# A ring of two small query tiles in place of two big ones, and one more row sum, in a fused attention backward pass

## The chip, the cores and the metric

The kernel runs on one core of a Trainium2 chip. A core has a matrix engine (PE; its weight loads are listed as PEld), a vector engine (DVE), a scalar engine (ACT), a general engine (POOL), and SyncE (SP), which here only issues transfers. Each works through its own list of instructions in order and waits at semaphores for the others. Transfers are carried out by 16 DMA engines that all queues share.

The metric is the device time of one execution in microseconds (us). A profiled execution gives two numbers: the span, from the first to the last instruction, and its own device time, which adds what lies around the span.

## What is computed

The reference is a forward pass of two attention blocks side by side and its gradient with respect to all eight inputs. S = 2048 tokens, D = 448, H = 16 heads of Dh = 28.

```python
# block A: linear attention, phi(t) = (t + 1 if t > 0 else exp(t)) + 1e-6
# block B: softmax attention with one key and value head for all 16 query heads
q = (x @ wq).reshape(B, S, H, Dh).transpose(0, 2, 1, 3);  k = x @ wk;  v = x @ wv
scores = einsum("bhqd,bkd->bhqk", q, k) * Dh ** -0.5
p = softmax(scores);  o = einsum("bhqk,bkd->bhqd", p, v)
out = concat([A(...), o.transpose(0, 2, 1, 3).reshape(B, S, H * Dh) @ wo], axis=-1)
# outputs: out, and the gradients of A_x, A_wqkv, A_wo, B_x, B_wq, B_wk, B_wv, B_wo
```

What follows concerns the backward pass of block B. With E = exp(scores), l the row sums of E, and dO the gradient of o: dP = dO vT, dS = E/l * (dP - D), where D is the row sum of dO * o. Then dQ = dS k, dK = dS^T q, dV = (E/l)^T dO.

## The kernel before

The kernel has two stages. The first (block A, and the projections of block B) takes about the first 200 us. The second is the core of block B, a loop over units u = 0 .. NU+27 with NU = 512 (lines 931 to 1049), and then a tail with the weight gradients and dX (lines 1051 to 1128). The order of the instructions inside the loop is the program's order; nothing reorders them.

A block b (64 of them) is a chunk of 256 queries, qc = b // 8, by a pair of heads, b % 8; two blocks share a group g of four heads. A unit is one eighth of a block: 256 of the 2048 keys, for two heads. Unit u does the scores S of block u // 8 and, 16 units behind, the dP of unit w = u - 16:

- `rows_SD` (L683) does the matmuls of S(u) and dP(w). ACT takes both halves of exp(S) into `eT` (L955, L997) and copies the second half of dP to `cp` (L971). DVE multiplies the first half of dP with `eT` into `dsT` (L967), POOL the second half (L972).
- After every fourth unit SP transposes four units of `eT` into `eN` with one DMA transpose of 128 x 4096 elements (L999). `dv_mm` (L901) reads `eN` for dV: block b in units 8b+20, 8b+22 and 8b+24. `eT` is a ring of five such tiles, `eN` of six.
- DVE transposes `dsT` in blocks of 32 into `dsx` (L1041), and `dk_m` (L865) multiplies it with the transposed queries `qX` for dK. Block b does so in the odd units 8b+27 to 8b+33.
- `o_norm` (L823) makes `rl` = 1/l and `don` = dO/l; its column 0 of each head carries D/l, which `row_D` (L833: one DVE reduction of `prod`, two small POOL multiplications) writes in unit 8b+12. `don_T` (PE, unit 8b+14) transposes `don` into `doT`, the operand of dP. A constant -1 in the values makes the matmul subtract D.
- dQ of block b is written over the block's queries in `qT_B`, in unit 8b+27 (L986).

The transposed queries. `qX` holds one 256-query chunk for all 16 heads, 128 x 8 x 512 elements, in two tiles that take turns (pools `cqXa` and `cqXb`). It is made group by group: `qc_copy` (L854, two calls for the even and the odd queries) spreads one group's queries into a staging tile, each repeated four times, and `qc_T` (L859) has SP transpose that, 128 x 1024 elements, into a quarter of `qX`. Chunk 0 is made ahead of the loop (L924 to L930), with `dsT` tiles as staging, one copy on POOL and one on DVE per group. Chunk c > 0 is made during the units of chunk c - 1: group g is copied by POOL in units 64(c-1) + 29 + 8g and the next one, into the single staging tile `qst`, and transposed at the end of the second. So in units 64(c-1)+29 to 64(c-1)+54 there is one group every 8 units, in the other units of a chunk there is none, and there is none from unit 448 on.

`row_D` is called inside `if hasD` (L963), which holds from unit 16 on. For block 0 it would be due in unit 12, so it isn't called, and column 0 of `don` stays what `o_norm` wrote, which is zero: block 0 is computed without D.

SP's list in the loop, in order: the load of `wo` (L923); the four transposes of chunk 0; then `eN` after every fourth unit; eight small transfers `put_shift` in unit 11 (L632); the transposes into `qX`; the transposes of `do_nat` into `oTq` (L1048) in units 130, 258, 386, 450 and 514. From unit 512 on `post_load` (L761, called at L1014) loads what the tail needs into `eT` tiles that are done: grad_out rows first (L775), then x rows (L780). `gwo` (L783), which starts in unit 520 on PE, multiplies with these rows; it is the last thing that PE does in its unit.

Of the kernel before, what the change touches and what calls it, by code (L numbers as in the profile page):

```python
# [11 lines left out]
BF16 = mybir.dt.bfloat16  # L12
# [5 lines left out]
P = 128  # L18
# [7 lines left out]
def kernel(  # L26
# [21 lines left out]
    nc = tc.nc  # L48
# [602 lines left out]
    with ExitStack() as cs_:  # L651
        pe_ = cs_.enter_context(tc.tile_pool(name="ceT", bufs=1, side="right"))
        pn_ = cs_.enter_context(tc.tile_pool(name="ceN", bufs=1, side="right"))
        pd_ = cs_.enter_context(tc.tile_pool(name="cdsT", bufs=5, side="right"))
        pqa_ = cs_.enter_context(tc.tile_pool(name="cqXa", bufs=1, side="right"))
        px_ = cs_.enter_context(tc.tile_pool(name="cdsx", bufs=2, side="right"))
        pqb_ = cs_.enter_context(tc.tile_pool(name="cqXb", bufs=1, side="right"))
        pc_ = cs_.enter_context(tc.tile_pool(name="ccp", bufs=3, side="right"))
        pw_ = cs_.enter_context(tc.tile_pool(name="cwk", bufs=4, side="right"))
        pp_ = cs_.enter_context(tc.tile_pool(name="cout", bufs=2, side="right"))  # L660
# [4 lines left out]
        dsT, dsx, qX, don, doT, rl, prod = ({} for _ in range(7))  # L665
# [3 lines left out]
        def eT(u):  # L669
            return ETs[u // 4 % 5][:, u % 4, :, :]  # L670
# [4 lines left out]
        def mmt(out, lhsT, rhs, pos, start, stop):  # L675
            nc.tensor.matmul(out, lhsT=lhsT, rhs=rhs, start=start, stop=stop, tile_position=pos,  # L676
                             skip_group_check=True)

        def blk(b):
            qc, pair = divmod(b, 8)  # L680
            return qc, pair, pair // 2, pair % 2
# [27 lines left out]
        qst = pp_.tile([P, 8, 4, 32], BF16, name="qst", bufs=1)[:, :, :, :]  # L709
# [92 lines left out]
        def due(u, lag):  # L802
            b, r = divmod(u - lag, 8)
            return b if r == 0 and 0 <= b < NB else None
# [28 lines left out]
        def row_D(b):  # L833
            Dq = pw_.tile([P, 2, 2, 1], F32, name="Dq")
            nc.vector.tensor_reduce(out=Dq[:, :, :, 0], in_=prod[b][:], axis=AX.X, op=ALU.add)
            nc.gpsimd.tensor_tensor(out=Dq[:], in0=Dq[:], in1=rl[b][:], op=ALU.mult)
            nc.gpsimd.tensor_tensor(out=don[b][:, :, :, 0:1], in0=Dq[:], in1=rl[b][:], op=ALU.mult)
# [13 lines left out]
            doT[b] = pw_.tile([P, 256], BF16, name="doT", bufs=2)  # L851
            nc.vector.tensor_copy(out=doT[b][r:r + 64, :], in_=tps2.pop(b)[r:r + 64, 0:256])  # L852

        def qc_copy(eng, st, qc, g, s):  # L854
            src = qT_B[g][:, qc * 256:(qc + 1) * 256].rearrange("p (b j s) -> p b j s", b=4, s=2)[:, :, :, s]
            eng.tensor_copy(out=st.rearrange("p (b s) a j -> p b s a j", s=2)[:, :, s, :, :],  # L856
                            in_=src.unsqueeze(2).to_broadcast([P, 4, 4, 32]))

        def qc_T(st, qc, g):  # L859
            nc.sync.dma_start_transpose(qX[qc].rearrange("p b s c -> p (b s) c")[:, :, g * P:(g + 1) * P],  # L860
                                        st.rearrange("p n a j -> p (n a j)"))

        dk_two = SB[2]

        def dk_m(b, m, other=0):  # L865
            qc, pair, g, hp = blk(b)
            h, B, s = m // 8, (m // 2) % 4, m % 2
            for a in range(4):
                rhs = dsx[b][32 * a:32 * a + 32, :, h, :, :].rearrange(
                    "p u t (b i s) -> p u t b i s", b=4, s=2)[:, :, :, B, :, s]  # L870
                k = 32 * ((a + 2) % 4) if other else 32 * a
                mmt((dk_two if other else dk_acc)[k:k + 32, :],
                    qX[qc][32 * a:32 * a + 32, B, s, pair * 64 + 32 * h:pair * 64 + 32 * h + 32],
                    rhs, (32 * a, k), other == 2 or b == 0 and m == 0, other == 0 and b == NB - 1 and m == 15)

        def o_mm(v):
# [44 lines left out]
        do_slots.update({32 + 8 * n: (13 + n // 4, n % 4 * P, n % 4 * P + P) for n in range(12)})  # L921
        with tc.manual_schedule():
            nc.sync.dma_start(wo, wo_d[:, 0:D].rearrange("(g p) c -> p g c", p=P))  # L923
            qX[0] = pqa_.tile([P, 4, 2, 512], BF16, name="qX")  # L924
            for g in range(4):
                st = pd_.tile([P, 2, 512], BF16, name="dsT").rearrange("p a (n j) -> p a n j", j=32).rearrange(
                    "p a (n b) j -> p (a n) b j", b=4)
                qc_copy(nc.gpsimd, st, 0, g, 0)
                qc_copy(nc.vector, st, 0, g, 1)
                qc_T(st, 0, g)  # L930
            for u in range(NU + 28):
                w = u - 16
                hasS = u < NU
# [5 lines left out]
                if u % 2 == 0:  # L939
                    b, n = divmod(u - 20, 8)  # L940
# [22 lines left out]
                if hasD:  # L963
                    dst = pd_.tile([P, 2, 512], BF16, name="dsT")
                    dsT[w] = dst
                    ew = eT(w)
                    nc.vector.tensor_tensor(out=dst[:, 0, :], in0=dp[0][:, :], in1=ew[:, 0, :], op=ALU.mult)  # L967
                    if (b := due(u, 12)) is not None:
                        row_D(b)
                    cp = pc_.tile([P, 512], BF16, name="cp")  # L970
                    nc.scalar.activation(out=cp[:, :], in_=dp[1][:, :], func=ACT.Copy)  # L971
                    nc.gpsimd.tensor_tensor(out=dst[:, 1, :], in0=cp[:, :], in1=ew[:, 1, :], op=ALU.mult)  # L972
                gq, iq = divmod(u % 64 - 29, 8)
                qq = u // 64 + 1
                if 0 <= gq < 4 and u < 448:
                    if gq == 0 and iq == 0:
                        qX[qq] = (pqb_ if qq % 2 else pqa_).tile([P, 4, 2, 512], BF16, name="qX")
                    if iq < 2:
                        qc_copy(nc.gpsimd, qst, qq, gq, iq)
                if u == 7:  # L980
                    nc.vector.memset(oTs[64:128, :], 0.0)
                if (b := due(u, 9)) is not None:
# [1 line left out]
                if (b := due(u, 27)) is not None:  # L984
                    qc, pair, g, hp = blk(b)
# [10 lines left out]
                if hasS:  # L996
                    nc.scalar.activation(out=eT(u)[:, 1, :], in_=sp[1][:, :], func=ACT.Exp, scale=scale)  # L997
                    if u % 4 == 3:
                        nc.sync.dma_start_transpose(ENs[u // 4 % 6][:, :, :],  # L999
                                                    ETs[u // 4 % 5][:, :, :, :].rearrange("p a b c -> p (a b c)"))  # L1000
                    if 0 <= gq < 4 and iq == 1 and u < 448:
                        qc_T(qst, qq, gq)

                if u % 2:
                    b, i = divmod(u - 27, 8)
                    if 0 <= b < NB:
                        for m in range(2 * i, 2 * i + 4):
                            dk_m(b, m, (1 + (u == 519 and m == 2 * i + 1)) * (m % 2) if 519 <= u < 537 else 0)
                else:
                    o_dq((u - 2, u - 1), (u - 20, u - 19))  # L1010
# [26 lines left out]
                if 0 <= y < NU:  # L1037
                    b, tp = divmod(y, 8)
                    if tp == 0:
                        dsx[b] = px_.tile([P, 8, 2, 2, 256], BF16, name="dsx")  # L1040
                    nc.vector.transpose(  # L1041
                        out=dsx[b][:, tp, :, :, :].rearrange("p h t c -> p (h t c)").bitcast(F32),
                        in_=dsT[y][:, :, :].rearrange("p h c -> p (h c)").bitcast(F32))
# [20 lines left out]
        for c in range(4):  # L1064
            t = dkvT[0:32, :].rearrange("p (t a i) -> p t a i", a=4, i=32)[:, :, c, :]
            src = dk_acc[32 * c:32 * c + 32, :].rearrange("p (t i) -> p t i", i=32)
# [93 lines left out]
```

## Time and profile before

| | us |
|---|---|
| median of 3 timed runs | 1042.17 (1039.36 to 1042.62) |
| device time of the profiled execution | 1044.09 |
| its span | 1042.4 |
| PE busy | 1003.5 (96%) |
| DVE, ACT, POOL busy | 886.9, 865.2, 812.3 |
| first exponential of the loop starts at | 207.09 |
| last exponential (unit 511) starts at | 969.45 |

The granted TensorE clock is full throughout. In a line of the profile that starts with a line number, the fields are: line, engine, operation, tiles written and read, shape, count, then busy time and the mean of one in ns, then the engine's idle time just before such instructions and what ended it. In a timeline the two numbers ahead of the engine are the start and the duration in us; SPq is SP's list of transfers, and a transfer's duration there is the time that SP takes to hand it over, not the time until it has landed.

### The profile page before, as it was taken

The numbers are of one execution on the slowest core, as the hardware profiler recorded it, in microseconds if no ns is written. First come the engines' busy times: TensorE is split into PE (matmuls) and PEld (weight loads), VectorE is DVE, ScalarE is ACT, GpSimd is POOL, SyncE is SP. The second block draws the span as 40 slices with busy tenths as digits, with TensorE's granted clock in tenths as the row PEclk, the third lists the DMA queues.
The fourth block names the chain that finished last, engine by engine and source line by source line (L and its number), as shares of the span: only waits on it lengthen the run. The fifth ranks groups of instructions, "written<-read, shape, count | busy, mean of one in ns | idle before, by whom it ended". The sixth has DMA issues, their size and how long they took to land.

```text
span 1042.4 us, 40109 instructions
## 1 busy us (share of the span) xinstructions
PE 1003.5 (96%) x16245; PEld 485.1 (47%) x16245; DVE 886.9 (85%) x1780; ACT 865.2 (83%) x1743; POOL 812.3 (78%) x1106
## 2 busy tenths in 40 slices
PE   9999999999999999999999999999999999999998
PEld 5555554434444444444444444444444444444444
DVE  7897500669999999999999999999999999999942
ACT  6463132599999999999999999999999999999632
POOL 8601282238998998999999989998999999889860
PEclk9999999999999999999999999999999999999999
DMA  9879999299999999999999999999999999999983
GB/s 261 157 137 191 176 229 218 38 161 201 194 187 192 187 193 194 202 187 194 201 193 195 192 187 204 198 182 202 188 197 186 195 195 195 200 188 203 228 168 90
DMA packets 689058, 195.15 MB, mean 187 GB/s; under 512 B 670408, under 2 KB 686688, under 8 KB 688872
## 3 DMA queue, kind: packets, MB, share of 16 engines
q1 hardware_dynamic: 680392, 179.97, 105.0%
q0 software_dynamic: 4544, 9.46, 3.0%
q10 hardware_dynamic: 3936, 3.16, 1.0%
q8 instruction: 127, 2.08, 0.8%
q14 instruction: 59, 0.48, 0.2%
HBM read 12.60 MB, written 10.84 MB: 22 GB/s over the span
## 4 chain that ended last, share of the span: by engine, by line
PE 39%; DVE 25%; POOL 16%; ACT 8%; issue 7%; DMA 3%; DVEq 0%; SPq 0%; ACTq 0%; POOLq 0%
PE agen L81 13%; POOL dsT L972 12%; DVE dsT L967 10%; PE agen L676 9%; DVE dsx L1041 9%; PE aacc L676 8%; PE aacc L81 7%; ACT cp L971 4%; ACT eT L997 2%; DMA eN<-eT 2%; DVE doT L852 1%; DVE R L986 1%; POOL qst L856 1%; POOL prod L821 1%; PE aacc L809 1%
## 5 line engine op out<-in xcount | busy, mean ns | idle before, releaser
L972 POOL TENSOR_TENSOR dsT<-cp,eT 128x512 bf16<-128x512 bf16 x512 | 584.6, 1156 | 49.4 <-ACT cp L971 42.6
L1041 DVE STREAM_TRANSPOSE dsx<-dsT 128x512 f32<-128x512 f32 x512 | 356.7, 697 | 5.8 <-POOL dsT L972 3.2
L676 PEld LDWEIGHTS <-R 32*128 32x128 bf16 (+1 forms) x9104 | 245.1, 94 | 243.3 <-issue 192.5
L967 DVE TENSOR_TENSOR dsT<-agen,eT 128x512 bf16<-128x512 f32 x512 | 340.3, 665 | 11.3 <-PE agen L676 5.4
L971 ACT ACTIVATE cp<-agen 128x512 bf16<-128x512 f32 x512 | 327.0, 639 | 11.8 <-PE agen L676 9.7
L955 ACT ACTIVATE eT<-aacc 128x512 bf16<-128x512 f32 x512 | 325.5, 636 | 12.0 <-PE agen L676 6.8
L997 ACT ACTIVATE eT<-aacc 128x512 bf16<-128x512 f32 x512 | 333.4, 651 | 0.0
L676 PE MATMUL agen<-dsx,qX 32*32 32x512 bf16 x4024 | 264.0, 376 | 0.0
L676 PE MATMUL agen<-doT,R 32*128 32x256 bf16 x2048 | 243.5, 269 | 4.1 <-DVE dsT L967 3.2
L676 PE MATMUL aacc<-R,R 32*128 32x256 bf16 (+1 forms) x2240 | 207.9, 267 | 16.7 <-DVE doT L852 6.6
L676 PE MATMUL agen<-dsT,R 128*32 128x256 bf16 x2048 | 155.5, 273 | 0.5 <-issue 0.5
L676 PE MATMUL agen<-eT,R 128*32 128x256 bf16 x2048 | 155.5, 273 | 0.1
L676 PEld LDWEIGHTS <-qX 32*32 32x32 bf16 x4096 | 78.3, 89 | 112.5 <-issue 54.1
L676 PE MATMUL aacc<-eN,don 128*32 128x512 bf16 x1024 | 91.7, 387 | 1.0 <-DMA eN<-eT 1.0
L81 PEld LDWEIGHTS <-R 128*128 128x128 bf16 x517 | 40.9, 98 | 41.0 <-issue 10.6
L81 PE MATMUL agen<-R,R 128*128 128x448 bf16 (+1 forms) x180 | 42.1, 361 | 0.3 <-DVE pq L244 0.3
L676 PEld LDWEIGHTS <-don 128*32 128x32 bf16 x1024 | 21.1, 93 | 42.5 <-issue 42.5
L856 POOL COPY qst<-R 128x512 bf16<-128x512 bf16 x56 | 34.2, 611 | 5.0 <-DVE dsx L1041 2.5
L821 POOL TENSOR_TENSOR prod<-R,oTs 128x128 f32<-128x128 bf16 x64 | 27.5, 430 | 9.0 <-DVE oTs L817 9.0
L586 DVE TENSOR_TENSOR osb<-R 32x512 bf16<-32x512 bf16 x4 | 1.7, 413 | 35.4 <-DMA R<-xa 33.8
L427 POOL COPY pk<-R 128x256 bf16<-128x256 bf16 x4 | 1.6, 399 | 37.7 <-DVE R L389 37.7
L262 POOL TENSOR_SCALAR wdq<-wdq 128x448 bf16<-128x448 bf16 x16 | 21.1, 1326 | 12.0 <-DVE phiT L243 12.0
(235 smaller groups left out, 1000.1 us busy)
## 6 DMA issues: line engine op xcount, KB each, us to landing
eN<-eT SPq DMA_TRANSPOSE x128
xa<-in_A_x_dram SPq DMA_DIRECT2D x8, 224.0 KB
ga<-in_grad_out_dram SPq DMA_DIRECT2D x4, 448.0 KB
out_dram<-osb ACTq DMA_DIRECT2D x16, 112.0 KB
xa<-in_grad_out_dram POOLq DMA_DIRECT2D x4, 448.0 KB, 7.1
out_dram<-wdq POOLq DMA_DIRECT2D x8, 224.0 KB, 5.5
eT<-in_grad_out_dram SPq DMA_DIRECT2D x4, 448.0 KB
eT<-in_B_x_dram SPq DMA_DIRECT2D x4, 448.0 KB
```

What stands on the lines that cost most here:

```text
L81: nc.tensor.matmul(out_ap, lhsT=lhsT, rhs=rhs, start=start, stop=stop, tile_position=(0, 0))
L262: nc.gpsimd.tensor_scalar(out=wq_n[:, st, 0:D], in0=wq_n[:, st, 0:D], scalar1=1.0, scalar2=None, op0=ALU.min)
L676: nc.tensor.matmul(out, lhsT=lhsT, rhs=rhs, start=start, stop=stop, tile_position=pos, skip_group_check=True)
L809: nc.tensor.transpose(onp[:, qb, :, :].rearrange("p h c -> p (h c)"), oTs[0:64, qb * P:(qb + 1) * P], identF[0:64, 0:64], tile_position=(0 ...
L821: nc.gpsimd.tensor_tensor(out=prod[b][:], in0=dnv, in1=os_, op=ALU.mult)
L856: eng.tensor_copy(out=st.rearrange("p (b s) a j -> p b s a j", s=2)[:, :, s, :, :], in_=src.unsqueeze(2).to_broadcast([P, 4, 4, 32]))
L955: nc.scalar.activation(out=eT(u)[:, 0, :], in_=sp[0][:, :], func=ACT.Exp, scale=scale)
L967: nc.vector.tensor_tensor(out=dst[:, 0, :], in0=dp[0][:, :], in1=ew[:, 0, :], op=ALU.mult)
L971: nc.scalar.activation(out=cp[:, :], in_=dp[1][:, :], func=ACT.Copy)
L972: nc.gpsimd.tensor_tensor(out=dst[:, 1, :], in0=cp[:, :], in1=ew[:, 1, :], op=ALU.mult)
L997: nc.scalar.activation(out=eT(u)[:, 1, :], in_=sp[1][:, :], func=ACT.Exp, scale=scale)
L1041: nc.vector.transpose(out=dsx[b][:, tp, :, :, :].rearrange("p h t c -> p (h t c)").bitcast(F32), in_=dsT[y][:, :, :].rearrange("p h c -> p ...
```

## The change

The two tiles of 512 columns become a ring of two tiles `qX` of 128 columns, one group each (pool `cqX`, bufs=2). A tile is made every 16 units: group G = u // 16 is copied by POOL in units 16G+13 and 16G+14 into `qst`, and transposed by SP at the end of the second, into the whole of a ring tile. `dk_m` reads tile b // 2. The four groups made ahead of the loop are gone, together with their use of DVE and of `dsT`; all 32 groups are now made in the loop, up to unit 510. `row_D(0)` is called in unit 12. The pools behind `cqX` move in memory, since the two old tiles took 16 KB of a partition and the ring takes 4 KB.

```diff
@@ -652,9 +652,8 @@
         pe_ = cs_.enter_context(tc.tile_pool(name="ceT", bufs=1, side="right"))
         pn_ = cs_.enter_context(tc.tile_pool(name="ceN", bufs=1, side="right"))
         pd_ = cs_.enter_context(tc.tile_pool(name="cdsT", bufs=5, side="right"))
-        pqa_ = cs_.enter_context(tc.tile_pool(name="cqXa", bufs=1, side="right"))
+        pq_ = cs_.enter_context(tc.tile_pool(name="cqX", bufs=2, side="right"))
         px_ = cs_.enter_context(tc.tile_pool(name="cdsx", bufs=2, side="right"))
-        pqb_ = cs_.enter_context(tc.tile_pool(name="cqXb", bufs=1, side="right"))
         pc_ = cs_.enter_context(tc.tile_pool(name="ccp", bufs=3, side="right"))
         pw_ = cs_.enter_context(tc.tile_pool(name="cwk", bufs=4, side="right"))
         pp_ = cs_.enter_context(tc.tile_pool(name="cout", bufs=2, side="right"))
@@ -851,14 +850,15 @@
             doT[b] = pw_.tile([P, 256], BF16, name="doT", bufs=2)
             nc.vector.tensor_copy(out=doT[b][r:r + 64, :], in_=tps2.pop(b)[r:r + 64, 0:256])
 
-        def qc_copy(eng, st, qc, g, s):
+        def qc_copy(G, s):
+            qc, g = divmod(G, 4)
             src = qT_B[g][:, qc * 256:(qc + 1) * 256].rearrange("p (b j s) -> p b j s", b=4, s=2)[:, :, :, s]
-            eng.tensor_copy(out=st.rearrange("p (b s) a j -> p b s a j", s=2)[:, :, s, :, :],
-                            in_=src.unsqueeze(2).to_broadcast([P, 4, 4, 32]))
-
-        def qc_T(st, qc, g):
-            nc.sync.dma_start_transpose(qX[qc].rearrange("p b s c -> p (b s) c")[:, :, g * P:(g + 1) * P],
-                                        st.rearrange("p n a j -> p (n a j)"))
+            nc.gpsimd.tensor_copy(out=qst.rearrange("p (b s) a j -> p b s a j", s=2)[:, :, s, :, :],
+                                  in_=src.unsqueeze(2).to_broadcast([P, 4, 4, 32]))
+
+        def qc_T(G):
+            qX[G] = pq_.tile([P, 4, 2, P], BF16, name="qX")
+            nc.sync.dma_start_transpose(qX[G].rearrange("p b s c -> p (b s) c"), qst.rearrange("p n a j -> p (n a j)"))
 
         dk_two = SB[2]
 
@@ -870,7 +870,7 @@
                     "p u t (b i s) -> p u t b i s", b=4, s=2)[:, :, :, B, :, s]
                 k = 32 * ((a + 2) % 4) if other else 32 * a
                 mmt((dk_two if other else dk_acc)[k:k + 32, :],
-                    qX[qc][32 * a:32 * a + 32, B, s, pair * 64 + 32 * h:pair * 64 + 32 * h + 32],
+                    qX[b // 2][32 * a:32 * a + 32, B, s, hp * 64 + 32 * h:hp * 64 + 32 * h + 32],
                     rhs, (32 * a, k), other == 2 or b == 0 and m == 0, other == 0 and b == NB - 1 and m == 15)
 
         def o_mm(v):
@@ -921,13 +921,6 @@
         do_slots.update({32 + 8 * n: (13 + n // 4, n % 4 * P, n % 4 * P + P) for n in range(12)})
         with tc.manual_schedule():
             nc.sync.dma_start(wo, wo_d[:, 0:D].rearrange("(g p) c -> p g c", p=P))
-            qX[0] = pqa_.tile([P, 4, 2, 512], BF16, name="qX")
-            for g in range(4):
-                st = pd_.tile([P, 2, 512], BF16, name="dsT").rearrange("p a (n j) -> p a n j", j=32).rearrange(
-                    "p a (n b) j -> p (a n) b j", b=4)
-                qc_copy(nc.gpsimd, st, 0, g, 0)
-                qc_copy(nc.vector, st, 0, g, 1)
-                qc_T(st, 0, g)
             for u in range(NU + 28):
                 w = u - 16
                 hasS = u < NU
@@ -965,18 +958,15 @@
                     dsT[w] = dst
                     ew = eT(w)
                     nc.vector.tensor_tensor(out=dst[:, 0, :], in0=dp[0][:, :], in1=ew[:, 0, :], op=ALU.mult)
-                    if (b := due(u, 12)) is not None:
+                    if u > 12 and (b := due(u, 12)) is not None:
                         row_D(b)
                     cp = pc_.tile([P, 512], BF16, name="cp")
                     nc.scalar.activation(out=cp[:, :], in_=dp[1][:, :], func=ACT.Copy)
                     nc.gpsimd.tensor_tensor(out=dst[:, 1, :], in0=cp[:, :], in1=ew[:, 1, :], op=ALU.mult)
-                gq, iq = divmod(u % 64 - 29, 8)
-                qq = u // 64 + 1
-                if 0 <= gq < 4 and u < 448:
-                    if gq == 0 and iq == 0:
-                        qX[qq] = (pqb_ if qq % 2 else pqa_).tile([P, 4, 2, 512], BF16, name="qX")
-                    if iq < 2:
-                        qc_copy(nc.gpsimd, qst, qq, gq, iq)
+                if u == 12:
+                    row_D(0)
+                if hasS and u % 16 in (13, 14):
+                    qc_copy(u // 16, u % 16 - 13)
                 if u == 7:
                     nc.vector.memset(oTs[64:128, :], 0.0)
                 if (b := due(u, 9)) is not None:
@@ -998,8 +988,8 @@
                     if u % 4 == 3:
                         nc.sync.dma_start_transpose(ENs[u // 4 % 6][:, :, :],
                                                     ETs[u // 4 % 5][:, :, :, :].rearrange("p a b c -> p (a b c)"))
-                    if 0 <= gq < 4 and iq == 1 and u < 448:
-                        qc_T(qst, qq, gq)
+                    if u % 16 == 14:
+                        qc_T(u // 16)
 
                 if u % 2:
                     b, i = divmod(u - 27, 8)
```

## The prediction, made before the changed kernel ran

> **What bounds the kernel now.** The page comes first: who is busy.
>
> ```profile
> PE 1003.5 (96%) x16245; PEld 485.1 (47%) x16245; DVE 886.9 (85%) x1780; ACT 865.2 (83%) x1743; POOL 812.3 (78%) x1106
> DMA  9879999299999999999999999999999999999983
> q1 hardware_dynamic: 680392, 179.97, 105.0%
> ```
>
> PE looks like the bound, but SP's queue q1 has had the DMA engines busy throughout as well. So the second view is SP's own list: the timeline of SP at the loop's start and at its end.
>
> ```profile
> 206.52 0.36 SPq L923 DMA_DIRECT2D wo<-wo_d  x1
> 208.41 5.38 SPq L860 DMA_TRANSPOSE qX<-dsT  x4
> 213.84 10.66 SPq L999 DMA_TRANSPOSE eN<-eT  x2
> 224.55 4.54 SPq L632 DMA_DIRECT2D R<-R  x8
> 229.18 26.77 SPq L999 DMA_TRANSPOSE eN<-eT  x5
> 256.05 1.26 SPq L860 DMA_TRANSPOSE qX<-qst  x1
> 257.41 11.04 SPq L999 DMA_TRANSPOSE eN<-eT  x2
> ...
> 954.98 21.94 SPq L999 DMA_TRANSPOSE eN<-eT  x4
> 977.02 1.07 SPq L775 DMA_DIRECT2D eT<-in_grad_out_dram  x2
> 978.18 3.06 SPq L1048 DMA_TRANSPOSE R<-R  x1
> ```
>
> The end of a row is the start of the next, within 0.1 us. Over the whole list from 208.41 to 977.02 the largest hole is 0.46 us. The first transpose of the loop starts at 213.84, though its last input (the exponential of unit 3) is there at 211.72; unit 455's is there at 885.51 and waits until 894.29. So the queue is never empty, and the load of grad_out rows behind the last transpose cannot be issued before 977.02, whatever the engines do.
>
> Third, the view of a single line, for the two lines that issue transposes: min, median and max ns of one, and who waits for it.
>
> ```profile
> L999 SPq DMA_TRANSPOSE eN<-eT x128: 4832/5440/6272, 213.8 to 971.0; - x128
> L860 SPq DMA_TRANSPOSE qX<-qst x28: 1235/1264/2050, 256.0 to 868.8; - x28
>   POOL qst L856: 2.5, 4
> ```
>
> The page's costliest groups say how long the engines waited.
>
> ```profile
> L856 POOL COPY qst<-R 128x512 bf16<-128x512 bf16 x56 | 34.2, 611 | 5.0 <-DVE dsx L1041 2.5 <-DMA qX<-qst 2.5
> L676 PE MATMUL aacc<-eN,don 128*32 128x512 bf16 x1024 | 91.7, 387 | 1.0 <-DMA eN<-eT 1.0
> ```
>
> They waited little for the queue: POOL 5.0 us, since `qst` is single (2.5 us are named, and the 2.5 put down to DVE, which was long done, are two more such waits), PE 1.0 us for `eN`.
>
> Fourth, PE's timeline at unit 520, the first `gwo`.
>
> ```profile
> 981.87 0.60 PE L676 MATMUL agen<-dsT,R 128*32 128x256 bf16 x8
> 982.63 0.92 PE L81 MATMUL aacc<-eT,R 128*128 128x448 bf16 x4 [0.16 <-DMA eT<-in_grad_out_dram]
> 983.48 0.39 PE L676 MATMUL agen<-doT,R 32*128 32x256 bf16 x4
> ```
>
> PE waits 0.16 us for the rows issued at 977.02, which land 5.6 us later. This is where the two chains meet: PE's own work and the queue arrive together. After it PE is nearly without holes to the end (the chain of the end is PE, with DVE steps of 0.6 us between).
>
> **The change part by part.** The sum is made against the profiled execution: span 1042.4, device time 1044.09. The timed median, 1042.17, is 1.92 us below that.
>
> *The queue.* Removed ahead of the loop: four transposes, 208.41 to 213.79, or 5.4 us. Added in the loop: four more (32 instead of 28), 4 x (1.264 + 0.1) = 5.5 us. The work is the same, its place isn't. Before, the four began at 208.41, and 3.4 us of them (208.41 to 211.8) lay where nothing else could be sent, since the first `eN` transpose has its input at 211.72. In the loop there is no hole to lie in. So all else on the queue is 2.0 us earlier at first (211.8 for 213.84), and after four more transposes 5.5 - 2.0 = **3.4 us later**: the last `eN` transpose ends at 980.3 instead of 976.9, the grad_out rows land at 986.0 instead of 982.6. PE has nothing to do in between, as its list is in order, and the tail goes with it: the x rows, the dQ transposes and the pads lie on the same queue, without a hole until 1016.7. That the first exponentials come earlier is excluded: ACT works without a hole from 207.09 to 211.71.
>
> How much of the 3.4 shows? Upper end 3.4: PE was already waiting. Lower end 1.6: if the 1.92 us by which timed runs are shorter all came from a faster queue, PE would be last there, with 1.8 us to cover. Loop and queue are tied (a stall of one lets the other catch up), so I take a small part off: **+3.1**.
>
> *A transpose's own price.* The new target is contiguous, the old one a quarter of a row. Nearest rows: the strided 256 KB take 1.264 us (207 GB/s); the contiguous 1 MB of `eN` takes 5.42 on average (693.6 / 128, 193 GB/s), a quarter of it 1.36. I take 1.264, the same block shape and size. Upper end 32 x 0.1 = 3.1 us more. Below, no row shows a cheaper block.
>
> [...]
>
> *The single staging tile.* Copies for a new group come 15 units after the last transpose instead of 7 (about 22 us for 10.3; eight units take 11.8). The transposes wait 5 to 10 us behind `eN`, so POOL's 5.0 us of waits go. What is late next: the queue still needs its time, so units that run earlier only lengthen the wait of `eN` in the queue, from 1 us at the end before to some 7. PE then waits for `eN` at `dv_mm`, 13 units behind the exponential. It did so when a transpose started 10.3 us after its input (unit 404, after the `oTq` transpose of 3 us in unit 386), so I expect 3 to 6 us of such waits, in and after units 258, 386 and 450. They cost nothing by themselves, as PE waits for the queue in unit 520 anyhow.
>
> *POOL and DVE.* Ahead of the loop POOL loses four copies (2.9 us) and DVE four (2.5 us): both ran beside ACT's first exponentials, and PE waited 0.3 us for a POOL row behind them. Gain 0 to 0.3, taken as 0, since the queue starts by ACT. In the loop POOL gets 8 more copies of 0.61 us: the first are in units 13 and 14, where POOL is idle until 227.85, and the last eight in units 461 to 510. Blocks of 8 units with copies and no wait take 11.80 us and those without 11.79, and in 874 to 970 POOL is busy 86 of 96 us, so it has room: 0. If that cover were gone, 8 x 0.61 = 4.9 us, on the engines' side and not the queue's.
>
> *Waits added.* SP's ring transpose waits for PE's reads of the tile two groups back, whose last is in unit 16G+9, and for POOL's copy of unit 16G+14; the `eN` of unit 16G+15 stands behind it. The queue is 5 us or more behind, so both are over: 0. PE reads a tile first in unit 16G+27, 13 units (19 us) after the copy; with 10 us in the queue, 1.3 to hand over and about 3.2 to land it is there: 0.
>
> *row_D(0).* One DVE reduction (0.275) and two POOL steps (0.20 and 0.22) in unit 12. DVE is idle 1.66 us ahead of 223.50 and POOL from 221.0 to 227.85; `don_T(0)` on PE at 223.72 comes after some 0.8 us to spare: 0. Without that cover 0.7 us, beside a queue that is behind by then.
>
> Sum: 3.1 us. Timed median 1042.17 + 3.1 = **1045.3** (a profiled execution 1047.2).
>
> **The rivals.**
>
> *The queue has room, and the change gains.* If in timed runs PE and not the queue is last at unit 520, the 5.0 + 1.0 us of waits go and nothing comes back: 1036 at best, about 1039 if they were half as large. It decides when the queue needs less than the engines: 3.4 + 6 = 9.4 us less in 768, an `eN` transpose at 5.35 instead of 5.42. For it: the timed runs are shorter than the profiled one, one at 1039.36. Against it: a median only 1.92 below. 13%.
>
> *A contiguous target is cheaper.* From 1.26 to 1.16 us per ring transpose the 3.4 us would be won back, from 0.97 down (9.4 us less in 32, as above) the queue is out of the way: 1036. Against it the 193 and 207 GB/s above. 4%. [...]
>
> *The tail takes it up.* PE's tail has waits for DVE and ACT of 0.2 to 0.4 us, some 1.5 in all; were they to vanish behind the later start, and the 1.8 be there too, about 1042.5. 10%.
>
> *The ring transposes cost what `eN` costs per byte*, 3.4 + 3.1: 1048.7. 10%.
>
> **How the numbers follow.** The forecast has 63%, its own range 1043.5 to 1046. 0.3% of 1042 is 3.1 us, about what a measurement of this kernel can tell from no change, and the forecast lies on that line: I give it 36 of its 63 points above and 27 below. Slower 36 + 10 = 46%; same 27 + 8 from the tail's case, 35%; faster 13 + 4 + 2, 19%. The range 1037.5 to 1049.5 leaves out the far side of both gains, and what exceeds the dearest case.
>
> **What would show it.** Right: SP's list has its first `eN` transpose at 211.8 and no hole until the grad_out load at about 980; PE's wait for `in_grad_out` in unit 520 is 3 to 8 us instead of 0.16; POOL's waits for `qX<-qst` are gone; PE's waits for `eN` grow from 1.0 to 3 to 6 us; 32 ring transposes take 1.26 us each. Wrong: holes in SP's list, or PE's wait in unit 520 still near zero.

## The result, and the profile after

The changed kernel takes 1047.57 us (median of 5 runs, 1046.05 to 1050.28), the kernel before in the same comparison 1042.23 (5 runs, 1039.36 to 1044.11). The ratio is **1.0054, 95% interval 1.0031 to 1.0077**: 5.3 us slower, between 3.2 and 8.0. The profiled execution has a span of 1046.1 (before 1042.4: 3.7 more) and a device time of 1047.83.

The page's busy times and SP's queue, after:

```profile
PE 1006.6 (96%) x16245; PEld 485.7 (46%) x16245; DVE 883.6 (84%) x1777; ACT 864.5 (83%) x1743; POOL 814.2 (78%) x1112
q1 hardware_dynamic: 680392, 179.97, 103.3%
```

DVE has 3.3 us less than before (2.5 of them are its four copies ahead of the loop), POOL 1.9 more and PE 3.1 more: none of the three tells where the loss lies. SP's list does, as before. Its timeline, at the loop's start and end:

```profile
206.56 0.36 SPq L923 DMA_DIRECT2D wo<-wo_d  x1
211.55 10.30 SPq L989 DMA_TRANSPOSE eN<-eT  x2
221.90 4.47 SPq L632 DMA_DIRECT2D R<-R  x8
226.49 5.00 SPq L989 DMA_TRANSPOSE eN<-eT  x1
231.59 1.25 SPq L861 DMA_TRANSPOSE qX<-qst  x1
...
972.30 1.30 SPq L861 DMA_TRANSPOSE qX<-qst  x1
973.69 5.80 SPq L989 DMA_TRANSPOSE eN<-eT  x1
979.60 1.08 SPq L774 DMA_DIRECT2D eT<-in_grad_out_dram  x2
980.72 1.44 SPq L1038 DMA_TRANSPOSE R<-R  x1
```

The 5.4 us of ring transposes that stood at 208.41 are gone and SP waits there, 4.6 us long, for the first exponentials. From 211.55 on the largest hole is 0.46 us, as before. The last `eN` transpose, handed over by 976.91 before, is now handed over at 979.49, and a ring transpose stands just ahead of it. The load of the grad_out rows is issued at 979.60 instead of 977.02: **2.6 us later**.

What PE does at unit 520, in its timeline after:

```profile
978.47 0.60 PE L675 MATMUL agen<-dsT,R 128*32 128x256 bf16 x8
983.60 1.65 PE L81 MATMUL aacc<-eT,R 128*128 128x448 bf16 x4 [4.53 <-DMA eT<-in_grad_out_dram]
985.18 0.61 PE L675 MATMUL agen<-doT,R 32*128 32x256 bf16 x4
```

PE comes to `gwo` 3.4 us earlier than before (978.47 for 981.87 in the row above it) and waits 4.53 us for the rows instead of 0.16. The rows are there only 1.0 us later than before (983.60 for 982.63), though: before, 15 of their 16 shares had landed by 981.07 and the last at 982.59; now all land between 982.93 and 983.55. Without that one late share PE, which was ready at 982.47, would have come last there before the change. The rest of the loss is in the second number of the row. The same four matmuls took 0.92 us before and take 1.65 here. The view by windows of 10 us says why; its columns are the window, its length, the busy time of PE, PEld, DVE, ACT and POOL, then the granted TensorE clock, the DMA share and GB/s. First before, then after:

```profile
980.00:990.00 10.00, 9.03 (x121) 3.80 (x121) 8.31 (x15) 5.59 (x11) 7.71 (x8) 1.00 1.18 262
```

```profile
970.00:980.00 10.00, 7.69 (x122) 3.43 (x117) 9.57 (x19) 4.06 (x8) 9.84 (x13) 1.00 1.26 212
980.00:990.00 10.00, 6.41 (x41) 1.99 (x41) 2.62 (x4) 2.24 (x4) 2.88 (x3) 0.52 1.11 286
990.00:1000.00 10.00, 9.62 (x124) 3.73 (x123) 7.00 (x12) 5.69 (x10) 5.28 (x5) 0.96 1.19 244
```

From 980.50 to 990.74 the clock is granted at half. The `dv` matmuls of unit 524, before and after:

```profile
988.52 0.61 PE L676 MATMUL aacc<-eN,don 128*32 128x512 bf16 x8
```

```profile
992.39 0.61 PE L675 MATMUL aacc<-eN,don 128*32 128x512 bf16 x8
```

So of 3.9 us, 1.0 are the later rows and **2.9 are the slow clock behind PE's wait**. The end of the span comes 3.7 us later, so the tail keeps it. Every run has its mean granted clock on record: it is 0.995 to 0.997 in the five runs of the changed kernel, and 0.998 to 1.000 in the 74 runs of the kernel before that stood beside the experiments below.

The groups of lines that waited, after:

```profile
L856 POOL COPY qst<-R 128x512 bf16<-128x512 bf16 x64 | 39.1, 612 | 5.2 <-DMA R<-R 5.2
L675 PE MATMUL aacc<-eN,don 128*32 128x512 bf16 x1024 | 91.7, 387 | 1.0 <-DMA eN<-eT 1.0
```

POOL no longer waits for `qX<-qst`. Its 5.2 us are the first copy alone, in unit 13, behind `put_shift`, where POOL had nothing else to do. The loop's last exponential starts at 966.05 instead of 969.45, and all of these 3.4 us are then lost at unit 520.

### The profile page after: what moved, and what is told of

It reads as the page before. It is cut to its first block, busy times and chain, and to the rows that moved or that the text cites. A ratio compares the mean times of both kernels' runs of the same rounds, so it can differ in the third digit from the quotient of the medians.

```text
span 1046.1 us, 40121 instructions
## 1 busy us (share of the span) xinstructions
PE 1006.6 (96%) x16245; PEld 485.7 (46%) x16245; DVE 883.6 (84%) x1777; ACT 864.5 (83%) x1743; POOL 814.2 (78%) x1112
## 4 chain that ended last, share of the span: by engine, by line
PE 43%; DVE 34%; ACT 9%; issue 7%; POOL 3%; DMA 3%; DVEq 0%; ACTq 0%; POOLq 0%
DVE dsT L960 14%; PE agen L81 13%; DVE dsx L1031 12%; PE agen L675 11%; PE aacc L675 9%; PE aacc L81 6%; ACT cp L964 4%; ACT eT L987 3%; POOL dsT L965 2%; DVE R L976 2%; DMA eN<-eT 2%; PE aacc L808 2%; DVE doT L851 2%; DVE Dq L834 1%; DVE oTs L816 1%
## 5 line engine op out<-in xcount | busy, mean ns | idle before, releaser
L856 POOL COPY qst<-R 128x512 bf16<-128x512 bf16 x64 | 39.1, 612 | 5.2 <-DMA R<-R 5.2
```

The costliest lines, as they stand in the source:

```text
L856: nc.gpsimd.tensor_copy(out=qst.rearrange("p (b s) a j -> p b s a j", s=2)[:, :, s, :, :], in_=src.unsqueeze(2).to_broadcast([P, 4, 4, 32]))
```

## The experiments

Theory after the result: SP's list sets when the rows land; the change moved work on that list from a place where it cost nothing (208 to 211.5) into the loop; and PE's wait behind it costs more than its length, because the clock drops. Rivals: the halved clock is only a mark of the wait; the ring's late place, not its amount, is the cause; the row sum D has a part in it. Ratios are to the kernel before, run beside it on the same chip.

**1. PE kept busy through the wait.** Eighteen matmuls whose result nobody reads, ahead of the first `gwo`:

```diff
+                if u == 520:
+                    for _ in range(18):
+                        mm(SB[0][:, :], identB[:, :], kT_rep[:, 0:512])
```

> The changed kernel, with 18 matmuls of 128x512 (0.215 us each, 3.9 us) put on PE in unit 520 ahead of the first gwo, into the bank that gwo starts fresh. Theory (the queue is late, PE idles 4.5 us for the grad_out rows, and the idle time halves the clock for 10 us): the rows land as before, at about 983.6, the idle time shrinks to under 1 us, the granted clock stays full, and units 520 and 521 take what they took in the kernel before: 2.9 us less than the changed kernel, about 1044.7. Rival (the halved clock costs nothing, or comes from something else): 1047.6, or up to 1 us more.

Measured: **1.0025 (1.0009 to 1.0041)**, median 1046.2. PE's timeline (it has 17 of the 18):

```profile
981.67 3.83 PE L81 MATMUL aacc<-R,identB 128*128 128x512 bf16 x17 [0.16 <-issue]
985.73 0.92 PE L81 MATMUL aacc<-eT,R 128*128 128x448 bf16 x4 [0.23 <-DMA eT<-in_grad_out_dram]
```

The rows come later here (985.73; the list ended at 981.70 in this execution), yet the four matmuls take 0.92 us again and the clock is full (1.00 from 980 to 990, and a mean of 1.000 in this execution). The span is 1.5 us shorter than the changed kernel's, though its rows were 2.1 us later. So the halved clock is a cost of its own: about 2.9 of the 5.4 thousandths by the medians. The two intervals overlap; what settles it are the durations of the same matmuls (1.65 and 0.92 us) and the mean clock, 0.998 to 1.000 in all ten runs. What is left, 2.5 thousandths, I put down to the list, since the wait is only filled here and not shortened; the next runs try that.

**2. The last four groups not transposed.** Groups 28 to 31 read the tile of group 27, so that dK lacks those groups' own queries, and SP has four transposes less in the last 64 units.

```diff
-                    if u % 16 == 14:
+                    if u % 16 == 14 and u < 448:
                         qc_T(u // 16)
+                    elif u % 16 == 14:
+                        qX[u // 16] = qX[27]
```

> The changed kernel without the ring transposes of groups 28 to 31 (their copies into qst stay); dk_m reads group 27's tile for them, so dK leaves those four groups' queries out. Theory (the work of SP's list in the last 64 units is what makes the grad_out rows late): the list ends 4 x 1.37 = 5.5 us earlier, at 974.0 instead of 979.5, the rows land near 978, just before PE wants them at 979.1, the clock stays full, and the time falls by 4.5 + 2.9 = 7.4 us to about 1 us (0.1%) under the kernel before. Rival (ring, layout or row sum cost by themselves): it stays near 0.5% above it.

Measured: **0.998 (0.996 to 1.0)**, median 1040.1 for 1042.92. In the profile PE has no wait for the rows in unit 520, and the clock stays full (its mean is 0.999 or 1.000 in all ten runs):

```profile
983.23 0.93 PE L81 MATMUL aacc<-eT,R 128*128 128x448 bf16 x4
```

Against the changed kernel's 1.0054 the four are worth 7.7 us (0.74% of 1042). The 5.1 us that they take on SP's list and the 2.9 us of the slow clock would make 8.0, but the profile bears out the clock alone: its last `eN` transpose ends at 978.04, where 974.0 was expected. This execution (1044.09) is one of the longer of the ten runs, with 4.9 us of waits for `eN` in the loop.

**3. The last four groups transposed twice.**

```diff
                     if u % 16 == 14:
                         qc_T(u // 16)
+                        if u // 16 >= 28:
+                            nc.sync.dma_start_transpose(qX[u // 16].rearrange("p b s c -> p (b s) c"),
+                                                        qst.rearrange("p n a j -> p (n a j)"))
```

> The changed kernel, with the ring transposes of groups 28 to 31 issued twice, 4 x 1.37 = 5.5 us more on SP's list. Theory: the list is never empty, so its end moves by 5.5 us to about 985, PE's wait in unit 520 grows from 4.5 to about 10 us, and the time by 5.5 us: about 1053. Rival (the list has room, PE's wait has another cause): 1047.6 to 1048.5.

Measured: 1.0158 (1.0135 to 1.0182). More than the transposes' own time: the second one writes the tile of the first and waits until that has landed (12.4 us in four waits of SP's queue for `qX<-qst`). SP's timeline, and PE's:

```profile
926.75 1.26 SPq L861 DMA_TRANSPOSE qX<-qst  x1
932.00 1.23 SPq L994 DMA_TRANSPOSE qX<-qst  x1
933.28 21.88 SPq L989 DMA_TRANSPOSE eN<-eT  x4
```

```profile
997.77 1.65 PE L81 MATMUL aacc<-eT,R 128*128 128x448 bf16 x4 [9.15 <-DMA eT<-in_grad_out_dram]
```

Here 928.01 to 932.00 is a hole of 4.0 us; the four holes are 12.7 us together, with 5 us of transposes beside them. The list ends at 993.63, 14.1 us later than in the changed kernel, PE waits 9.15 us with half the clock behind it (and 3.01 and 3.52 us for `eN` in the loop, with half the clock behind these too), and the span is 12.1 us longer. The holes make it no clean doubling, but what is put on the list late does show at the end.

**4. Two of the groups made ahead of the loop again.** Groups 0 and 1 are copied into `dsT` tiles and transposed before the loop, the ring is filled in the loop from unit 45 on.

```diff
+            for G in range(2):
+                st = pd_.tile([P, 2, 512], BF16, name="dsT").rearrange("p a (n j) -> p a n j", j=32).rearrange(
+                    "p a (n b) j -> p (a n) b j", b=4)
+                qc_copy(G, 0, nc.gpsimd, st)
+                qc_copy(G, 1, nc.vector, st)
+                qc_T(G, st)
...
-                    if u % 16 == 14:
+                    if u >= 32 and u % 16 == 14:
```

> The changed kernel, with groups 0 and 1 made ahead of the loop again (as the kernel before made its first four), the ring and all else unchanged. Theory: two transposes, 2.7 us, fit into the hole ahead of the first eN transpose (208.4 to 211.5), so SP's list ends 2.7 us earlier, near 976.8; the rows land near 980.8, PE waits under 2 us, and the time falls by 2.8 us, or by 5.6 if the clock then stays full: 1042 to 1044.8. Rival (where the groups are made does not matter): 1047.6.

Measured: **1.0051 (1.0027 to 1.0075)**, no gain. The theory as it stood fell here. SP's list began like the changed kernel's (first `eN` transpose at 211.51), with two fewer transposes to do, and its last `eN` transpose still ended at 978.83, 0.7 us earlier and not 2.7. PE waits 3.76 us for the rows, and the clock is at half for 10.24 us. The timeline of its start shows where the rest went:

```profile
208.05 2.66 SPq L861 DMA_TRANSPOSE qX<-dsT  x2
211.51 10.37 SPq L995 DMA_TRANSPOSE eN<-eT  x2
221.93 4.54 SPq L632 DMA_DIRECT2D R<-R  x8
226.56 48.38 SPq L995 DMA_TRANSPOSE eN<-eT  x9
276.44 1.31 SPq L861 DMA_TRANSPOSE qX<-qst  x1
```

Between 264 and 348 the list has holes (0.57, 0.71, 1.49, 0.68 and 0.79 us): SP had caught up with the exponentials and had nothing to send. In the loop's first quarter, from the fifth transpose on, the changed kernel's `eN` transposes start at least 1.6 us after the end of their last exponential and those of before at least 4.1; here some start at once. Time saved at the front is kept only if there is work to fill it. The ring of two, with a group every 16 units, had none.

**5. A ring of eight.** The 32 groups are spread over units 13 to 446, so that none falls in the last 64 units, as before the change; none is made ahead of the loop.

```diff
-        pq_ = cs_.enter_context(tc.tile_pool(name="cqX", bufs=2, side="right"))
+        pq_ = cs_.enter_context(tc.tile_pool(name="cqX", bufs=8, side="right"))
...
+            at13 = {8 * (7 * G // 4) + 13: G for G in range(32)}
```

> The changed kernel with a ring of eight tiles and the groups made every 14 units on average (units 8 * floor(7G/4) + 13 and 14), so that the last is made in unit 446 and the last 64 units have none, as in the kernel before. Theory: SP's list catches up in the last 64 units and ends near 975 to 977; the rows are in time or nearly so, and the time is that of the kernel before within 0.2%, though PE waits 3 to 6 us for eN around units 386 to 450. Rival (it is the making in the loop itself that costs): 0.5% above.

Measured: **1.005 (1.0034 to 1.0065)**; a miss. At the end it went nearly as wished: the last `eN` transpose ended at 978.45, and PE had no wait at unit 520. But the denser transposes put the list further behind in mid-loop (around unit 260 up to 11.4 us behind the exponentials, for 5.8 there in the changed kernel), and PE met an `eN` that wasn't there:

```profile
616.53 0.61 PE L675 MATMUL aacc<-eN,don 128*32 128x512 bf16 x6 [2.58 <-DMA eN<-eT]
```

2.58 us, and then the clock at half from 617.92 for 3.41 us. That does not account for the whole loss. This execution is 2.7 us under the median of its ten runs, and two of the others, with a mean clock of 0.999 and 1.000, took 1047.9 and 1048.68; where the rest goes is open. So the late place alone is not the cause either: with all 32 groups in the loop, the loss is there in both of the places tried.

**6. Both: a ring of eight, and two groups ahead of the loop.** The other thirty in units 13 to 446.

```diff
+            at13 = {8 * (15 * (G - 2) // 8) + 13: G for G in range(2, 32)}
```

> The changed kernel with a ring of eight groups: two groups copied and transposed ahead of the loop, the other thirty spread over units 13 to 446, so that SP's list has no ring transpose in the last 64 units and two fewer in the loop than the ring of eight alone. Theory: both late work and the wait in mid-loop of the ring of eight (2.58 us for one transpose of exponentials at 616.5, and a clock of 0.5 for 3.41 us behind it) go away; the last transpose of exponentials ends at 975 to 978, no wait for rows over 1 us, clock 1.0 throughout, time 0.998 to 1.001 of the kernel before. Rival: a loop without POOL's 5.0 us of waits runs up against SP's list wherever the ring's work is put; then TensorE waits 2 us or more for a transpose of exponentials somewhere between 500 and 900, the clock is halved there, and the time is 1.003 to 1.006.

Measured: **0.9995 (0.9978 to 1.0013)**, median 1042.89 for 1043.21: the loss is gone. SP's timeline at the end and PE's:

```profile
946.17 27.22 SPq L998 DMA_TRANSPOSE eN<-eT  x5
973.49 1.07 SPq L774 DMA_DIRECT2D eT<-in_grad_out_dram  x2
```

```profile
979.26 0.92 PE L81 MATMUL aacc<-eT,R 128*128 128x448 bf16 x4 [0.32 <-DMA eT<-in_grad_out_dram]
```

The wait in mid-loop is 1.19 us (at 615.11) and leaves the clock full. The two transposes at 208.3 to 211.0 lie where the list had nothing else to send, and the big ring, filled earlier, gives the list work in time to use what they saved: in the first quarter of the loop its `eN` transposes start, from the fifth on, at least 3.2 us behind the exponentials, and from 211.67 until the rows' load the list has no hole over 0.46 us. This is the working of the prediction, run backwards: 2.7 us of transposes put back into the idle 3.4 us, kept by the larger ring, undo the loss, and neither does it alone. The ring of eight takes the same memory in the last two runs, which differ by 5.5 thousandths, so the moved pools by themselves are not what costs. The row sums of block 0 are computed in it, so they cost nothing that shows.

**7. The ring alone, without the row sums of the first block.**

```diff
-                if u == 12:
-                    row_D(0)
```

> The changed kernel without row_D(0) in unit 12, so that the ring is tried alone; the first block's row sums are left uncomputed, as they were before the change. My price for them was 0: they lie in unit 12, 750 us ahead of the place where the list of SP and the halved clock set the end. Theory: same time as the changed kernel, 1.004 to 1.006 times the kernel before, rows of grad_out waited for 4 to 5 us, clock 0.5 for about 10 us behind it. Rival: the row sums hold DVE and POOL at the loop's start and through them every later unit; then 1.001 to 1.003, and the last exponential starts over 1 us earlier than 966.05.

Measured: **1.0052 (1.0033 to 1.007)**, the changed kernel's 1.0054 again. PE's wait for the rows is 3.81 us. In the profiled execution the clock was at half for 3.41 us only, and its span is 1.6 us shorter; the other eight runs have a mean clock of 0.995 to 0.997 (0.998 in this one), and the median of the nine, 1047.71, does not follow it. The last exponential starts at 967.18 instead of 966.05, the other way from what the rival asked for.

**8. The rows issued in other ways.** If the rows are what PE waits for, they, or the late transposes ahead of them, could go another way. None of four kernels brought the time back.

The four loads issued by ACT (`nc.scalar.dma_start` in line 774):

> The changed kernel, with the four loads of grad_out rows issued by ACT instead of SP, so that they do not stand behind the late transposes. Theory: the rows are there before PE reaches unit 520 (about 979.1), no wait and no halved clock: 4.5 + 2.9 = 7.4 us less than the changed kernel if nothing else on SP's list is late, about 1040.2, which is 2 us under the kernel before; if the x rows and dQ transposes, still on SP's list, are late next, 1041 to 1044. Rival (the layout, the wait of POOL in unit 13 or the added row sum is what costs): 1047.6.

Measured: 1.0055 (1.0027 to 1.0083). The first three loads go out at 969.94 to 975.85, while `eN` transposes are being moved, and the last `eN` is handed over at 987.02 instead of 979.49, 8.2 us after its start. ACT comes to its fourth load late (984.32), `cp` stands behind it, and PE waits there:

```profile
985.45 0.58 PE L675 MATMUL agen<-doT,R 32*128 32x256 bf16 x2 [3.94 <-ACT cp L964]
```

The clock is at half for 6.83 us. One wait has taken the other's place; the run says nothing on the rows alone.

The first two loads issued by SP in unit 511, ahead of the last `eN` transpose, and (second) this with the 14 pad loads of `wkvT` taken off SP's list and issued by ACT and POOL:

```diff
+                if u == 511:
+                    post_load(0)
+                    post_load(1)
...
-                if 512 <= u < 528 and u % 2 == 0:
+                if 516 <= u < 528 and u % 2 == 0:
```

> The changed kernel, with the first two loads of grad_out rows issued by SP in unit 511, just ahead of the last eN transpose instead of behind it; the list's work is the same. Theory: they are issued near 973.7 instead of 979.6 and land near 978, PE does not wait in unit 520, the clock stays full: up to 7.4 us less than the changed kernel. What is late next is the rest of the list, which ends no earlier (pads into qT_B until 1017.9), so PE may wait for those at the first dX and give 3 to 4 us back: between 0.2% under and 0.2% above the kernel before. Rival (the wait is not the list's order): 0.5% above.

> As the run with the rows first, and the 14 small loads of pad rows into wqT (7.4 us on SP's list) issued by ACT and POOL in turn. Theory: the rest of the list ends some 7 us earlier, so PE's tail does not wait for the pads either: 0.2 to 0.4% under the kernel before. Rival (the tail is bound by PE and the pads are in time anyway): the same as the run with the rows first.

Measured: 1.0045 (1.0021 to 1.0068), and 1.007 (1.0044 to 1.0096). In both PE reaches the first `gwo` early, as meant: 980.01 after a wait of 1.65 us, and 979.15 after none. The list gets no shorter by it. In the first the last `eN` transpose ends at 983.51, all that follows is late, the pads `R<-eN` are issued from 1017.19 to 1021.00 (in the changed kernel up to 1017.85), and PE, early, stands still for them:

```profile
1021.58 0.53 PE L81 MATMUL aacc<-eT,R 128*128 128x448 bf16 x1 [5.20 <-DMA R<-eN]
```

The clock is at half for 6.83 us around it. In the second PE waits 3.99 us at 1011.06, for ACT, again followed by half a clock (3.41 us); its runs spread from 1042.67 to 1055.93, for which I have no cause. Moving the rows within the list did not help in these two runs: in the first, the tail takes its next bite from the same list.

The transposes of groups 28 to 31 issued by ACT instead of SP, one unit later:

```diff
-            nc.sync.dma_start_transpose(qX[G].rearrange("p b s c -> p (b s) c"), qst.rearrange("p n a j -> p (n a j)"))
+            (nc.scalar if G >= 28 else nc.sync).dma_start_transpose(qX[G].rearrange("p b s c -> p (b s) c"), qst.rearrange("p n a j -> p (n a j)"))
...
```

> The changed kernel with the transposes of the last four groups (28 to 31) issued by ACT, one unit later, and not by SP. SP's list has 5.1 us less in the last 64 units, as when these four were left out, and every output is still whole. Theory of the late list: the last transpose of exponentials ends at 974 to 978 and not at 979.5, TensorE waits under 1 us for the rows of grad_out, the clock stays at 1.0, and the time is 0.997 to 1.001 of the kernel before. Rival: ACT, busy 99 percent of every stretch of the loop, is held by each issue for its 1.26 us or more; the last exponential then starts 3 to 6 us later than 966.05, and the time is 1.001 to 1.006, with the wait for rows gone all the same.

Measured: **1.024 (1.0203 to 1.0277)**, four times the loss that the dearer of the two theories allowed. ACT's timeline, and the waits of SP's queue:

```profile
900.94 1.34 ACTq L861 DMA_TRANSPOSE qX<-qst  x1
902.33 0.60 ACT L948 ACTIVATE eT<-aacc 128x512 bf16<-128x512 f32 x1 [9.34 <-issue]
```

```profile
SPq L989 <- DMA qX<-qst: 22.9, 4, 6.6
```

ACT stands at its transpose for 8 us until those of SP have landed, and SP then waits for ACT's to land, 22.9 us in four such waits, the longest 6.6: in this run the transposes of the two queues followed each other, and both sides waited. What sets these waits, and what would happen without them, was not tried.

## Why the prediction was right, and where not

Forecast 1045.3, range 1037.5 to 1049.5, slower likeliest; measured 1047.57, slower, within the range. The forecast's own range, 1043.5 to 1046, missed it: the sum was 3.1, and it was 5.3 by the medians, 3.7 by the profiled executions. That the sum came as near as it did is in part luck: the rows were 1.0 us later and not 3.4, and a cost that it did not have added 2.9.

- *The queue.* Right in direction and place, off in size. Four transposes gone from 208.41, a first `eN` transpose at 211.55 (forecast 211.8), no hole over 0.46 us until the rows' load, all as forecast. The load came at 979.60, where 980.3 was forecast: +2.6 for +3.4, since the start was 0.25 us earlier and the transfers took some 0.6 us less in all. The rows were expected 3.1 to 3.4 us later and came 1.0 later, because the 5.6 us between issue and landing before held a straggler: one of 16 shares came 1.5 us after the others. It took 3.95 us this time. I had read one landing as a fixed lag. The last `eN` transpose starts 7.0 us behind its exponential instead of 0.95, as forecast ("from 1 us at the end before to some 7"): before, with no ring transposes in the last 64 units, the list had all but caught up there.
- *"PE has nothing to do in between"* is where the prediction failed. It named a wait of 3 to 8 us in unit 520 (4.53), and costed it by its length alone. The clock at half for 10.24 us behind it cost 2.9 us more and hid, in the sum, how much less the rows were late. The trace before could have warned of it only by its full clock, having no wait of that size (its longest in the loop is 1.01 us). In the trace after, the clock was lowered at 980.50, 1.4 us after the wait of 4.53 us had begun; in the ring of eight's a wait of 2.58 us was followed by half the clock too, for 3.41 us.
- *What the timed runs add.* The profiled execution of the changed kernel stands at the median of its runs (1047.83 and 1047.57); that of before stands 1.9 us above its own. I took that difference as a reason for less than 3.4. The two medians are 5.3 apart, 1.6 more than the spans, and what the runs without a profile did differently is open.
- *A transpose's own price.* Right: 32 ring transposes at a median of 1264 ns, to the nanosecond that of the strided ones. The second rival (a contiguous target is cheaper) is out: 207 GB/s, both ways. The fourth (the price of `eN` per byte, 1.36 us) is out too.

```profile
L861 SPq DMA_TRANSPOSE qX<-qst x32: 1231/1264/2217, 231.6 to 972.3; - x32
L989 SPq DMA_TRANSPOSE eN<-eT x128: 4812/5432/6147, 211.6 to 973.7; - x128
```

- *The single staging tile.* POOL's 5.0 us went, and the loop ran 3.4 us faster, to no effect. The expected 3 to 6 us of waits for `eN` did not come (1.0): the list was some 11 us behind the exponentials at most. That waits for `eN` are free, since PE has to wait in unit 520 anyhow, did not hold everywhere: the ring of eight, in its traced execution, paid for one of 2.58 us, with 3.41 us of half the clock behind it.
- *POOL, DVE, waits added, row_D(0)* at 0: right for the row sums (1.0052 without, 1.0054 with them). The others were not tried one by one, and no wait in the trace speaks against them.
- *The queue has room* (13%): out, though not as far as I thought. Two transposes fewer in the loop bring out 4.2 us of holes between 264 and 348. The changed kernel's list is 1.6 to 6.2 us behind the exponentials in the loop's first quarter, and 6.2 to 11.1 in its last, where it counts. *The tail takes it up* (10%): out, the end moved by as much as unit 524.

## What to carry to other kernels

Work on the in-order transfer list was free here only where the list would else have been empty (2.7 us of transposes in the idle time up to 211.7, with the ring of eight, experiment 6); ask of each moved transfer what stood idle at its old place, and then of each us gained whether there is work ready to fill it. A wait on TensorE had two prices here, its length and the slow clock behind it: look at the granted clock by windows, and cost a long wait with something on top (2.9 us behind a wait of 4.53; behind a wait of 1.65 the clock was full, behind one of 2.58 it was half). Where two engines arrive as close to each other as here (PE waited 0.16 us for the rows in unit 520 before), a gain of one alone can show nothing (POOL's 5.0 us of waits did not), and a loss of the other shows at once (the rows, 1.0 us later).

## What the runs showed of the hardware that I had not expected

- The clock: waits of TensorE of 1.01 us (the kernel before, at 243.5), 1.19 (experiment 6) and 1.65 (experiment 8, the rows first) left it full. Others were followed by half the clock: for 3.41 us those of 2.58 (experiment 5), 3.01 and 3.52 (experiment 3), 3.81 (experiment 7) and 3.99 us (experiment 8, with the pads moved); for 6.83 us those of 3.94 and 5.20 (experiment 8, the rows by ACT and the rows first); for 10.24 us those of 3.76 (experiment 4), 4.53 (the changed kernel) and 9.15 (experiment 3). These stretches are one, two and three times 3.41 us, and the wait's length alone doesn't tell which: 3.76 us brought 10.24, 3.99 us brought 3.41. The half clock began 1.4 us after the wait's begin in the changed kernel, and 1.4 us after its end in the ring of eight (617.92, for a wait that ended at 616.53). What tells more is where a wait falls: in the traces of the two kernels all changes of the clock lie whole multiples of 3.413 us apart (304 of them before; 286, 3 and 16 after), so they stand on a grid. Of the stretches of this grid at full clock, those right ahead of a halving had TensorE busy for 0.05 of the time (before, as its work ended), and for 0.47 and 0.12 (after, at 977.08 and, as its work ended, at 1041.93); all others had it busy for at least 0.65. The two traces have no stretch in between, and no run tried one.
- Landing is not handing over: the same load of rows, issued by SP behind the last `eN` transpose, landed 3.95 us after its issue in the changed kernel, and 5.57 us after it in the kernel before, where one of 16 shares came 1.5 us behind the others. PE, which waited for it, began its matmuls 3.9 and 4.0 us after the issue in experiments 1 and 3, and 5.8 us after it in experiment 6.
- In experiment 3 a transpose that writes the tile of the one before it held SP's list for 1.9 to 4.0 us until that had landed. In experiment 8 a transpose on ACT's queue held ACT 8 us, and SP 6.6 us at most.
- The kernel before has runs from 1039.5 to 1047.3 (31 on one chip), so one profiled execution can be 4 us from the median; single spans here, such as 1038.6 for the last version and 1044.5 without the row sums, mean little.
